# A convolution and a maxout layer on one core: both products in 64-row tiles of the array, side by side

## The chip, the core and the metric

The kernel runs on one core of a Trainium2 chip. The metric is the time of one execution on the device in microseconds (us); less is better. A core has five engines that run on their own queues: TensorE (PE, the products; its weight loads are listed as PEld), VectorE (DVE), ScalarE (ACT), GpSimd (POOL) and SyncE (SP, here only for issuing transfers). TensorE writes its products to PSUM, eight banks of 512 f32 columns on 128 partitions; VectorE and ScalarE read PSUM; everything else lies in SBUF.

## The reference

```python
# x: (8, 4160, 192), weight: (8 heads, 7 taps), moe_w1..3: (192, 768), moe_w_out: (768, 192)
w = softmax(weight, axis=-1)
x_pad = concat([zeros(B, 6, D), x], axis=1)
conv = einsum('hk,bskhg->bshg', w, windows_of_7(x_pad))     # causal, one filter per head of 24 channels
y = conv.reshape(33280, 192)
h = maximum(maximum(y @ w1, y @ w2), y @ w3)
out = h @ w_out                                             # (33280, 192) float32
```

## The kernel before

The 33280 tokens are cut into 65 blocks of 512 (`NBLK`); a block from the end of the eight sequences is put together from eight pieces of 64 tokens. Channels lie on partitions, tokens on columns. All products are in f16, with sums in f32.

The maximum is rewritten. With d1 = w1 - w3 and d2 = w2 - w3, max(y w1, y w2, y w3) is max(relu(y d1), y d2) + y w3, and the last term goes through w_out without a nonlinearity, as y m with m = w3 w_out. So l1, the first stage, needs two products in place of three, and st2, the second, adds y m to h w_out.

For each block t:

- `load_x` (issued on SP) brings x in chunks of 128 rows that overlap by 6 (122 new tokens each), and `cast_x` (GpSimd, L127) makes them f16.
- `conv` (L221): each chunk is multiplied with a band matrix of one head's taps, eight heads, five chunks, 40 products. Each works in one 128-row, 32-column tile of the array (`tile_position`). Two PSUM banks `G0`, `G1` hold four heads each. A head has 24 channels and takes a slot of 32 partitions, so the 192 channels fill two half tiles of 128 partitions, in which 8 of 32 rows of weights are zeros. ScalarE copies both banks to f16 (`y`, L228).
- `l1(t, j)` (L238) for six chunks j of 128 columns of the 768: two PSUM banks, for d1 and d2, and for each the two half tiles of channels in turn: 4 products of 128 rows and 512 columns. ScalarE takes relu of the first bank (`r`, L241), VectorE the maximum of r and the second bank (`h`, L242). Two buffers for each bank.
- `st2(t, s)` for four slices s of 128 tokens: two products y m (L253) and six h w_out (L256), 128 rows and 192 columns each, summed in one bank; two slices share a bank, and VectorE copies them out (L259).
- `store` (L268, L273) is issued on SP.

The order of the work is written out by hand, and engines take their instructions in that order. In a block's turn TensorE does l1 chunk 0, the conv of the next block, l1 chunk 1, and then in turn a slice of st2 of the block before and an l1 chunk, to chunk 5. In the first block's turn `make_m` computes m, with w3 transposed on TensorE in f32 (L198, L204). Ahead of that: the taps go to a band through a DRAM buffer `Rd` (L137 to L154); w1, w2, w3 come in pieces of 24 rows into the slots (L167, L170), w1 and w2 through ScalarE's queue, w3 through SP's, and are subtracted (`wd`, L186).

## Time and profile before

| | |
|---|---|
| median of 3 runs | 598.8 us (597.6 to 599.57) |
| the profiled execution | 599.25 us; its span in the trace 597.4 us |
| TensorE, VectorE, ScalarE, GpSimd busy | 94%, 57%, 50%, 12% of the span |
| mean granted TensorE clock | 0.997 |
| bytes moved by DMA | 61.40 MB, mean 103 GB/s |

The profile is one execution. A row of the groups names a line of the kernel, an engine, an operation, the tiles written and read, and a count; then the busy time in us and the mean duration of one in ns; then the idle time of the engine just before these instructions and what ended it. Records of matmuls overlap, since the next begins while the last drains, so the sum of their durations is more than the time that they take. The chain is followed back from the last instruction, at each step to what released it. A timeline row has a start and a length in us, an engine (ACTq and SPq are the issuing of a transfer), a line, an operation and a count of merged instructions.

### The profile page before, as it was taken

What the parts mean: (1) busy time and instruction counts of PE and PEld (TensorE: products, weight loads), DVE (VectorE), ACT (ScalarE), POOL (GpSimd) and SP (SyncE); (2) the same over time, 40 slices, a digit from 0 to 9 for tenths busy, and PEclk for the clock granted to TensorE, in tenths of its full rate; (3) what the DMA queues carried; (4) which work ended last, traced back from release to release, by engine and by line L of the source; (5) the groups of instructions that cost most, each with busy time, mean ns of one, the idle gap of its engine ahead of it and who ended that gap; (6) DMA issues with size and microseconds to landing.
All of it is one profiled execution on the core that took longest, in us unless ns stands there. A gap on an engine that the chain in (4) does not pass through costs nothing.

```text
span 597.4 us, 15039 instructions
## 1 busy us (share of the span) xinstructions
PE 562.2 (94%) x6300; PEld 361.1 (60%) x6300; DVE 342.9 (57%) x542; ACT 299.2 (50%) x523; POOL 72.0 (12%) x95
## 2 busy tenths in 40 slices
PE   0199999999999999999999999999999999999995
PEld 0066666666666666666666666666666666666663
DVE  1645656555655565556555656565555656565663
ACT  1135555555555555555555555555555555555551
POOL 2200111101111011101101111011101110111100
PEclk9999999999999999999999999999999999999998
DMA  7502432333234323442344334323443343324211
GB/s 206 172 1 61 119 109 83 109 120 112 83 105 120 114 87 100 121 118 83 98 121 120 86 94 120 120 87 92 121 121 89 91 119 112 103 86 118 83 55 53
DMA packets 79107, 61.40 MB, mean 103 GB/s; under 512 B 2912, under 2 KB 78208, under 8 KB 79040
## 3 DMA queue, kind: packets, MB, share of 16 engines
q1 hardware_dynamic: 78032, 58.43, 33.3%
q10 hardware_dynamic: 1008, 2.02, 1.0%
q8 instruction: 49, 0.80, 0.6%
q14 instruction: 18, 0.15, 0.1%
HBM read 34.34 MB, written 26.09 MB: 101 GB/s over the span
## 4 chain that ended last, share of the span: by engine, by line
PE 94%; DMA 3%; DVE 1%; ACT 1%; ACTq 0%; issue 0%; SPq 0%
PE l L238 58%; PE pso L256 22%; PE pso L253 7%; PE G L221 6%; DMA xf<-in_x_dram 1%; PE pm L204 1%; DMA ws<-in_moe_w_dram 1%; DMA wk<-in_weight_dram 1%; DMA Rd<-R 1%; ACTq L170 0%; DVE h L242 0%; DVE ws L167 0%; ACT r L241 0%; ACT wo L189 0%; SPq L116 0%
## 5 line engine op out<-in xcount | busy, mean ns | idle before, releaser
L238 PE MATMUL l<-y,wd 128*128 128x512 f16 x1560 | 392.4, 381 | 9.0 <-ACT y L228 9.0
L242 DVE TENSOR_TENSOR h<-r,l 128x512 f16<-128x512 f16 x390 | 268.2, 688 | 224.8 <-ACT r L241 220.4
L241 ACT ACTIVATE r<-l 128x512 f16<-128x512 f32 x390 | 234.1, 600 | 235.2 <-PE l L238 235.2
L238 PEld LDWEIGHTS <-wd 128*128 128x128 f16 x1560 | 143.8, 98 | 121.2 <-DVE wd L186 9.6
L256 PE MATMUL pso<-wo,h 128*128 128x192 f16 x1560 | 171.4, 246 | 0.4 <-DVE h L242 0.4
L256 PEld LDWEIGHTS <-h 128*128 128x128 f16 x1560 | 132.7, 98 | 0.6 <-DVE h L242 0.6
L127 POOL CAST x<-xf 128x960 f16<-128x960 f32 (+3 forms) x88 | 70.0, 800 | 487.3 <-DMA xf<-in_x_dram 358.0
L253 PEld LDWEIGHTS <-y 128*128 128x128 f16 x520 | 50.8, 98 | 60.7
L253 PE MATMUL pso<-m,y 128*128 128x192 f16 x520 | 85.4, 246 | 0.0
L228 ACT CAST y<-G 128x512 f16<-128x512 f32 x130 | 69.8, 589 | 28.0 <-PE G L221 28.0
L259 DVE COPY o<-pso 128x384 f32<-128x384 f32 x130 | 71.6, 551 | 1.8 <-PE pso L256 1.8
L221 PEld LDWEIGHTS <-x 128*32 128x32 f16 (+2 forms) x2624 | 36.6, 98 | 45.5 <-issue 40.0
L221 PE MATMUL G<-band,x 128*32 128x122 f16 (+3 forms) x2624 | 43.1, 211 | 18.4 <-DVE band L154 18.4
L189 ACT CAST wo<-wos 128x1152 f16<-128x1152 f32 x1 | 1.2, 1152 | 21.6 <-DMA ws<-in_moe_w_dram 21.6
L154 DVE COPY band<-bandc 128x1072 f16<-128x1072 f16 x1 | 2.5, 2530 | 9.5 <-DMA bandc<-Rd 9.5
L186 DVE TENSOR_TENSOR wd<-ws,ws 128x768 f16<-128x768 f32 x4 | 3.8, 959 | 4.2 <-DMA ws<-in_moe_w_dram 4.2
L204 PE MATMUL pm<-wos,w3t 128*128 128x192 f32 x24 | 4.2, 330 | 0.0
L204 PEld LDWEIGHTS pm<-wos,w3t 128*128 128x128 f32 x24 | 3.9, 190 | 0.2 <-DVE w3t L199 0.2
L167 DVE MEMSET ws<- 128x1536 f32 x2 | 2.7, 1338 | 0.5 <-issue 0.3
L206 DVE CAST m<-pm 128x192 f16<-128x192 f32 x2 | 0.7, 357 | 3.1 <-PE pm L204 3.1
L198 PE MATMUL pt<-ident,ws 128*128 128x128 f32 x12 | 1.7, 277 | 0.7 <-DVE w3t L199 0.7
L141 DVE TENSOR_REDUCE wsum<-wexp 128x8 f32<-128x56 f32 x1 | 0.3, 251 | 3.2 <-ACT wexp L139 3.2
(14 smaller groups left out, 8.9 us busy)
## 6 DMA issues: line engine op xcount, KB each, us to landing
out_dram<-o SPq DMA_DIRECT2D x64, 384.0 KB
xf<-in_x_dram SPq DMA_DIRECT2D x48, 480.0 KB
xf<-in_x_dram SPq DMA_DIRECT2D x16, 384.0 KB
ws<-in_moe_w_dram ACTq DMA_DIRECT2D x16, 72.0 KB
xf<-in_x_dram SPq DMA_DIRECT2D x8, 96.0 KB
ws<-in_moe_w_dram SPq DMA_DIRECT2D x8, 72.0 KB
wos<-in_moe_w_out_dram SPq DMA_DIRECT2D x1, 576.0 KB
xf<-in_x_dram SPq DMA_DIRECT2D x8, 70.5 KB
```

The costliest lines, as they stand in the source:

```text
L127: nc.gpsimd.tensor_copy(out=x16[0:rl, q0:q1, :], in_=xf[0:rl, q0:q1, :])
L167: eng.memset(st[:], 0.0)
L186: nc.vector.tensor_sub(out=d16[:, half, :], in0=wa[:, half, :], in1=w3s[:, half, :])
L204: nc.tensor.matmul(ps[:], lhsT=w3t[:, j, half, :], rhs=wos[:, j, :], start=(j == 0), stop=(j == NJ - 1))
L221: nc.tensor.matmul(G[h // 4][32 * g:32 * g + 32, lo:hi], lhsT=x16[0:rlen, q, cb:cb + 32], rhs=band[0:rlen, h, cc:cc + hi - lo], start=True ...
L228: nc.scalar.copy(out=y[:, i, 0:N], in_=G[i][:, 0:N])
L238: nc.tensor.matmul(ps[i][:, 0:N], lhsT=wd[i][:, half, P * j:P * (j + 1)], rhs=y[:, half, 0:N], start=(half == 0), stop=(half == 1))
L241: nc.scalar.activation(out=r[:, 0:N], in_=ps[0][:, 0:N], func=AF.Relu)
L242: nc.vector.tensor_max(out=hs[t][:, j, 0:N], in0=r[:, 0:N], in1=ps[1][:, 0:N])
L253: nc.tensor.matmul(ps[:, s % 2, :], lhsT=y[:, half, sl], rhs=m16[:, half, :], start=(half == 0), stop=False)
L256: nc.tensor.matmul(ps[:, s % 2, :], lhsT=hT[:, j, sl], rhs=wo[:, j, :], start=False, stop=(j == NJ - 1))
L259: nc.vector.tensor_copy(out=outs[t][0][:, s - 1:s + 1, :], in_=ps[:])
```

## The change

- The 192 channels are three groups of 64. An array tile of 64 rows takes one group, and the array has two such tiles, on partitions 0 to 63 and 64 to 127. In l1 the upper half holds d1 and the lower d2 (`wd` is one tensor now): three products each, taken in turn, into two banks.
- st2's sum over rows is split between the halves into two banks (`po0`, `po1`): h's rows 0 to 63 and 64 to 127 of each of six chunks, and three products y m shared out so that two slices have 15 products each, 8 on one half and 7 on the other, changing sides. ScalarE copies one bank to SBUF (`a`) and VectorE adds the other to it, in place of one copy.
- The conv's slots have to be packed to dense groups of 64 and be there twice, on both halves. The conv's result goes to `ys` for two blocks together; ten transfers on SP move the pieces of heads to the upper half of `yd`, and one on GpSimd copies the upper half to the lower (`repack`). The first block's pieces go on three queues, twice each, without the duplicate; the second block is packed alone.
- The conv runs four blocks ahead (`AHEAD`) in place of one; four convs, `make_m` and two groups' repack now stand ahead of the first l1, and in a turn the conv of block t+4.
- Stores are issued on GpSimd. x has three f32 buffers, not four; r has four. PSUM: `psp` and `psq` two banks each for l1, `psw` four banks shared by the conv and st2.
- The band is made from a zeroed DRAM buffer into which only the taps are written; half of the copy that turns it is ScalarE's. Weights come in four transfers of 64 rows on SP (w3 twice), and there are three subtractions, not four. `make_m` has the dense layout, its transposes in 64-row tiles.

On TensorE, l1 chunk 4 of a block begins so before (`l0` and `l1` are the banks for d1 and d2, `wd0` and `wd1` the weights):

```order
L238 LDWEIGHTS wd0_161
L238 MATMUL l0_46_4_6883<-y_46_6683,wd0_161 128x512
L238 LDWEIGHTS wd0_161
L238 MATMUL l0_46_4_6883<-y_46_6683,wd0_161 128x512
L238 LDWEIGHTS wd1_164
L238 MATMUL l1_46_4_6884<-y_46_6683,wd1_164 128x512
```

In the changed kernel an l1 chunk ends and st2 begins so on TensorE (`lp` and `lq` are the two banks of l1, `po0` and `po1` those of st2):

```order
L273 LDWEIGHTS wd_146
L273 MATMUL lp_32_1_6632<-yd_17_6045,wd_146 128x512
L273 LDWEIGHTS wd_146
L273 MATMUL lq_32_1_6633<-yd_17_6045,wd_146 128x512
L303 LDWEIGHTS yd_16_5658
L303 MATMUL po0_31_0_6643<-m16_154,yd_16_5658 128x192
L303 LDWEIGHTS yd_16_5658
L303 MATMUL po1_31_0_6644<-m16_154,yd_16_5658 128x192
```

Before, one bank was filled and then the other; now the banks take turns from product to product, in both stages.

On ScalarE, a block's turn before, from the last chunk of the block ahead of it:

```order
L241 ACTIVATE r_39_5_5909<-l0_39_5_5903 128x512
L241 ACTIVATE r_40_0_5925<-l0_40_0_5919 128x512
L228 CAST y_41_5970<-G0_41_5928 128x512
L228 CAST y_41_5970<-G1_41_5929 128x512
L241 ACTIVATE r_40_1_5979<-l0_40_1_5973 128x512
L241 ACTIVATE r_40_2_5997<-l0_40_2_5991 128x512
L241 ACTIVATE r_40_3_6015<-l0_40_3_6009 128x512
```

And in the changed kernel (`ys` is the conv's result in slots, `a` the copy of st2's first bank):

```order
L277 ACTIVATE r_31_0_6385<-lp_31_0_6377 128x512
L231 CAST ys_18_6242<-G0_35_6388 128x512
L231 CAST ys_18_6242<-G1_35_6389 128x512
L277 ACTIVATE r_31_1_6452<-lp_31_1_6444 128x512
L277 ACTIVATE r_31_2_6480<-lp_31_2_6472 128x512
L307 COPY a_30_1_6498<-po0_30_0_6455 128x384
L277 ACTIVATE r_31_3_6509<-lp_31_3_6501 128x512
L277 ACTIVATE r_31_4_6537<-lp_31_4_6529 128x512
L307 COPY a_30_3_6555<-po0_30_2_6512 128x384
L277 ACTIVATE r_31_5_6566<-lp_31_5_6558 128x512
```

The two casts of the conv stay between chunk 0 and chunk 1; two copies `a` are new, behind chunks 2 and 4.

GpSimd had only casts before. In the changed kernel its queue over two blocks is (`yd<-yd` is the duplicate, `out_dram<-o` a store):

```order
L133 CAST x_12_1717<-xf_1527 128x960
L260 DMA yd_1776<-yd_1776 64x3072
L317 DMA out_dram<-o_1532 128x4x192
L133 CAST x_13_1916<-xf_1715 128x960
L317 DMA out_dram<-o_1720 128x4x192
```

Each duplicate stands between a cast and a store, and each cast behind a store.

The core of the diff:

```diff
-    xfp = ctx.enter_context(tc.tile_pool(name="xfp", bufs=4))
+    xfp = ctx.enter_context(tc.tile_pool(name="xfp", bufs=3))
...
+    ysp = ctx.enter_context(tc.tile_pool(name="ysp", bufs=2))
+    ydp = ctx.enter_context(tc.tile_pool(name="ydp", bufs=4))
+    rp = ctx.enter_context(tc.tile_pool(name="rp", bufs=4))
     hp = ctx.enter_context(tc.tile_pool(name="hp", bufs=2))
+    tp = ctx.enter_context(tc.tile_pool(name="tp", bufs=2))
...
-    psg = ctx.enter_context(tc.tile_pool(name="psg", bufs=1, space=bass.MemoryType.PSUM))
-    psl = ctx.enter_context(tc.tile_pool(name="psl", bufs=2, space=bass.MemoryType.PSUM))
-    pst = ctx.enter_context(tc.tile_pool(name="pst", bufs=2, space=bass.MemoryType.PSUM))
+    psp = ctx.enter_context(tc.tile_pool(name="psp", bufs=2, space=bass.MemoryType.PSUM))
+    psq = ctx.enter_context(tc.tile_pool(name="psq", bufs=2, space=bass.MemoryType.PSUM))
+    psw = ctx.enter_context(tc.tile_pool(name="psw", bufs=4, space=bass.MemoryType.PSUM))
+    groups = [[0], [1]] + [list(range(t, min(t + 2, NB))) for t in range(2, NB, 2)]
+    group_of = {t: (g, k) for g, ts in enumerate(groups) for k, t in enumerate(ts)}
+    AHEAD = 4
...
+    zero = const.tile([P, BW], FP16)
+    nc.vector.memset(zero[:], 0.0)
+    Rd = dram.tile([P, BW], FP16)
+    nc.scalar.dma_start(out=Rd[:], in_=zero[:])
...
+    taps = const.tile([P, KW, NHEAD], FP16)
...
+        nc.vector.tensor_mul(out=taps[:, KW - 1 - k, :], in0=wexp[:, k, :], in1=wrec[:])
+    nc.scalar.dma_start(
+        out=bass.AP(tensor=Rd[:].tensor, offset=Rd[:].offset,
+                    ap=[[BW + NHEAD, P], [1, KW * NHEAD]]),
+        in_=taps[:].rearrange("p k h -> p (k h)"))
...
+    nc.scalar.dma_start(out=bandc[:].rearrange("p c h -> p (c h)"), in_=Rd[:])
...
+    HALF, NC = 64, D // 64
+    ws = const.tile([P, NC, DFF], FP32)
+    w3s = const.tile([P, NC, DFF], FP32)
+    for (lo, st, wsrc) in ((0, ws, moe_w1), (0, w3s, moe_w3), (HALF, ws, moe_w2), (HALF, w3s, moe_w3)):
+        nc.sync.dma_start(out=st[lo:lo + HALF, :, :], in_=wsrc.rearrange("(c r) f -> r c f", r=HALF))
...
+    wd = const.tile([P, NC, DFF], FP16)
+    for c in range(NC):
+        nc.vector.tensor_sub(out=wd[:, c, :], in0=ws[:, c, :], in1=w3s[:, c, :])
+    band = const.tile([P, NHEAD, BAND_W], FP16)
+    hh = NHEAD // 2
+    nc.vector.tensor_copy(out=band[:, 0:hh, :].rearrange("p h c -> p c h"), in_=bandc[:, :, 0:hh])
+    nc.scalar.copy(out=band[:, hh:NHEAD, :].rearrange("p h c -> p c h"), in_=bandc[:, :, hh:NHEAD])
...
+            for k in range(2):
+                js = slice(P * (2 * g + k), P * (2 * g + k + 1))
+                for c in range(NC):
+                    nc.tensor.transpose(ps[:, k, HALF * c:HALF * (c + 1)], w3s[0:HALF, c, js],
+                                        ident[0:HALF, 0:HALF])
+            nc.vector.tensor_copy(out=w3t[:, 2 * g:2 * g + 2, 0:D], in_=ps[:])
+            nc.vector.tensor_copy(out=w3t[:, 2 * g:2 * g + 2, D:2 * P], in_=ps[:, :, P:D])
...
+        G = [psw.tile([P, NBLK], FP32, tag="w", name=f"G{i}_{t}") for i in range(2)]
...
-        y = yp.tile([P, 2, NBLK], FP16, tag="y", name=f"y_{t}")
+        g, k = group_of[t]
+        if k == 0:
+            slots[g] = ysp.tile([P, 2, 2 * NBLK], FP16, tag="ys", name=f"ys_{g}")
         for i in range(2):
-            nc.scalar.copy(out=y[:, i, 0:N], in_=G[i][:, 0:N])
-        ys[t] = y
+            nc.scalar.copy(out=slots[g][:, i, NBLK * k:NBLK * k + N], in_=G[i][:, 0:N])
         xin.pop(t)
...
+    def repack(t):
...
+        if t >= NB or t != groups[group_of[t][0]][-1]:
+            return
+        g, k = group_of[t]
+        yd = dense[g] = ydp.tile([P, NC, 2 * NBLK], FP16, tag="yd", name=f"yd_{g}")
+        w = slice(0, NBLK * (k + 1))
+        if g == 0:
+            qs = (nc.sync, nc.scalar, nc.gpsimd)
+            todo = [(lo, p) for p in pieces for lo in (0, HALF)]
+            for n, (lo, (half, s0, c, r0, rows)) in enumerate(todo):
+                qs[n % 3].dma_start(out=yd[lo + r0:lo + r0 + rows, c, w],
+                                    in_=slots[g][s0:s0 + rows, half, w])
+            return
+        for (half, s0, c, r0, rows) in pieces:
+            nc.sync.dma_start(out=yd[r0:r0 + rows, c, w], in_=slots[g][s0:s0 + rows, half, w])
+        nc.gpsimd.dma_start(out=yd[HALF:P, :, w], in_=yd[0:HALF, :, w])
...
     def l1(t, j):
         N = blkN[t]
-        y = ys[t]
-        ps = [psl.tile([P, NBLK], FP32, tag=f"l{i}", name=f"l{i}_{t}_{j}") for i in range(2)]
-        for i in range(2):
-            for half in range(2):
-                nc.tensor.matmul(ps[i][:, 0:N], lhsT=wd[i][:, half, P * j:P * (j + 1)],
-                                 rhs=y[:, half, 0:N], start=(half == 0), stop=(half == 1))
+        g, k = group_of[t]
+        y = dense[g]
+        ps = [pool.tile([P, NBLK], FP32, tag=tag, name=f"l{tag}_{t}_{j}")
+              for pool, tag in ((psp, "p"), (psq, "q"))]
+        for c in range(NC):
+            for i in range(2):
+                row = slice(HALF * i, HALF * (i + 1))
+                nc.tensor.matmul(ps[i][:, 0:N], lhsT=wd[row, c, P * j:P * (j + 1)],
+                                 rhs=y[row, c, NBLK * k:NBLK * k + N],
+                                 start=(c == 0), stop=(c == NC - 1))
         r = rp.tile([P, NBLK], FP16, tag="r", name=f"r_{t}_{j}")
         nc.scalar.activation(out=r[:, 0:N], in_=ps[0][:, 0:N], func=AF.Relu)
         nc.vector.tensor_max(out=hs[t][:, j, 0:N], in0=r[:, 0:N], in1=ps[1][:, 0:N])
...
-        y, hT = ys[t], hs[t]
-        sl = slice(P * s, P * (s + 1))
+        g, k = group_of[t]
+        hT, y = hs[t], dense[g]
         if s % 2 == 0:
-            outs[t][1] = pst.tile([P, 2, D], FP32, tag="pso", name=f"pso_{t}_{s}")
-        ps = outs[t][1]
-        for half in range(2):
-            nc.tensor.matmul(ps[:, s % 2, :], lhsT=y[:, half, sl], rhs=m16[:, half, :],
-                             start=(half == 0), stop=False)
-        for j in range(NJ):
-            nc.tensor.matmul(ps[:, s % 2, :], lhsT=hT[:, j, sl], rhs=wo[:, j, :],
-                             start=False, stop=(j == NJ - 1))
+            halves[t] = [psw.tile([P, 2, D], FP32, tag="w", name=f"po{i}_{t}_{s}")
+                         for i in range(2)]
+        ps = halves[t]
+        tok = slice(NBLK * k + P * s, NBLK * k + P * (s + 1))
+        todo = []
+        for i in range(2):
+            row = slice(HALF * i, HALF * (i + 1))
+            mm = [(y[row, i, tok], m16[row, 0, :])]
+            if s % 2 == i:
+                mm.append((y[row, 2, tok], m16[row, 1, :]))
+            mm += [(hT[row, j, P * s:P * (s + 1)], wo[row, j, :]) for j in range(NJ)]
+            todo.append(mm)
+        for n in range(NJ + 2):
+            for i in range(2):
+                if n < len(todo[i]):
+                    nc.tensor.matmul(ps[i][:, s % 2, :], lhsT=todo[i][n][0], rhs=todo[i][n][1],
+                                     start=(n == 0), stop=(n == len(todo[i]) - 1))
         if s % 2 == 1:
-            nc.vector.tensor_copy(out=outs[t][0][:, s - 1:s + 1, :], in_=ps[:])
+            a = tp.tile([P, 2, D], FP32, tag="a", name=f"a_{t}_{s}")
+            nc.scalar.copy(out=a[:], in_=ps[0][:])
+            nc.vector.tensor_add(out=outs[t][:, s - 1:s + 1, :], in0=a[:], in1=ps[1][:])
     def store(t):
         if t < 0:
             return
-        ob = outs.pop(t)[0]
+        ob = outs.pop(t)
...
+                nc.gpsimd.dma_start(out=out[g0:g0 + n, :].rearrange("(s p) c -> p s c", p=P),
...
     assert all(n == NBLK for n in blkN)
-    conv(0)
-    for t in range(NB + 1):
-        if t < NB:
+    for t in range(AHEAD):
+        conv(t)
+        repack(t)
+        if t + 3 <= AHEAD + 1:
             load_x(t + 3)
-            cast_x(t + 2)
-            hs[t] = hp.tile([P, NJ, NBLK], FP16, tag="h", name=f"h_{t}")
-            outs[t] = [outp.tile([P, 4, D], FP32, tag="o", name=f"o_{t}"), None]
-            l1(t, 0)
-            conv(t + 1)
-            l1(t, 1)
-            for j in range(2, NJ):
-                st2(t - 1, j - 2)
-                l1(t, j)
-            if t == 0:
-                make_m()
-        else:
-            for s in range(4):
-                st2(t - 1, s)
+        if t + 3 <= AHEAD:
+            cast_x(t + 3)
+        if t == 1:
+            make_m()
+    for t in range(NB):
+        load_x(t + AHEAD + 2)
+        cast_x(t + AHEAD + 1)
+        hs[t] = hp.tile([P, NJ, NBLK], FP16, tag="h", name=f"h_{t}")
+        outs[t] = outp.tile([P, 4, D], FP32, tag="o", name=f"o_{t}")
+        l1(t, 0)
+        conv(t + AHEAD)
+        repack(t + AHEAD)
+        l1(t, 1)
+        for j in range(2, NJ):
+            st2(t - 1, j - 2)
+            l1(t, j)
         store(t - 1)
+    for s in range(4):
+        st2(NB - 1, s)
+    store(NB - 1)
```

More of the change, by code (lines that the diff above doesn't have):

```diff
@@ L194, in make_m @@
         for g in range(NJ // 2):
[L195 to L202 removed]
+            ps = psq.tile([P, 2, D], FP32, tag="q", name=f"pt{g}")
@@ L214, in conv @@
         N = blkN[t]
-        G = [psg.tile([P, NBLK], FP32, tag=f"g{i}", name=f"G{i}_{t}") for i in range(2)]
+        G = [psw.tile([P, NBLK], FP32, tag="w", name=f"G{i}_{t}") for i in range(2)]
         x16 = xin[t][1]
```

68 lines of the change are left out of this document (18 added, 50 removed).

## The prediction

> **What bounds the kernel now.** I read the page first: who is busy, and whose work makes up the chain that ended last.
>
> ```profile
> PE 562.2 (94%) x6300; PEld 361.1 (60%) x6300; DVE 342.9 (57%) x542; ACT 299.2 (50%) x523; POOL 72.0 (12%) x95
> PE 94%; DMA 3%; DVE 1%; ACT 1%; ACTq 0%; issue 0%; SPq 0%
> GB/s 206 172 1 61 119 109 83 109 120 112 83 105 120 114 87 100 121 118 83 98 121 120 86 94 120 120 87 92 121 121 89 91 119 112 103 86 118 83 55 53
> ```
>
> TensorE is 94% of the chain, DMA 3%. The stretches of the span say whether TensorE ever pauses in the middle (its columns: length, TensorE busy, weight loads, VectorE, ScalarE, GpSimd, clock, DMA share, GB/s):
>
> ```profile
> 100.00:580.00 480.00, 480.00 (x5428) 307.77 (x5427) 285.56 (x452) 256.95 (x451) 57.99 (x75) 1.00 0.35 102
> ```
>
> 480.00 of 480 us at clock 1.00: no gap. A busy matmul row overlaps its neighbour, so the real price of one is read from the chain in order of time, one block of 512 tokens long (start, length, work):
>
> ```profile
> 51.25 1.73 PE l L238 x8
> 52.98 0.58 PE G L221 x40
> 53.56 0.97 PE l L238 x4
> 54.53 0.17 PE pso L253 x2
> 54.69 0.49 PE pso L256 x6
> 55.19 0.86 PE l L238 x4
> ...
> 59.76 1.73 PE l L238 x8
> ```
>
> A block takes 59.76 - 51.25 = 8.51 us. A 512-column product costs 1.73/8 = 0.216 us, a 192-column one (0.17 + 0.49)/8 = 0.0825 us, the conv's 40 small products 0.58 us, and there is 0.97 - 0.86 = 0.11 us behind the conv. Sum: 24 x 0.216 + 32 x 0.0825 + 0.58 + 0.11 = 5.18 + 2.64 + 0.69 = 8.51. TensorE's stream is the bound, and nothing else.
>
> **TensorE's work after.** One l1 chunk had 4 products in turn; now it has 6 of 64 rows, three on each half of the array: if the two halves run side by side, 3 x 0.216 = 0.65 us instead of 0.86. One st2 slice had 8 products in turn, now 15 in two halves, 7.5 x 0.0825 = 0.62 us instead of 0.66. The conv keeps its shape, and the array changes its tile shape twice in a block as before. Sum: 18 x 0.216 + 30 x 0.0825 + 0.69 = 3.89 + 2.48 + 0.69 = **7.05 us**, 1.46 less.
>
> No row shows 64-row tiles. The nearest is the conv: 40 products of up to 122 columns, four column tiles, in 0.58 us, 58 ns for a round of four. At 0.0825 us for 192 columns one such product alone is about 0.052 us, so four at once cost about 6 ns more than one. Bounds for a pair: 1.0 to 2.0 products; I take 1.0, the row that is nearest. The Trainium skill, *TensorE: Matmul & The Clock Gate*, "Measured speedup vs the span model", gives 3.07 for four row tiles, not 4; a pair at that efficiency would cost 1.30 products and the block, by estimate, 8.97 us. By it this change loses (the second rival); the trace agrees only in part: the conv's row shows 4 x 52/58 = 3.6 of four, though of column tiles.
>
> The second unknown is weight loads: 136 in a block instead of 96. The groups by shape:
>
> ```profile
> L238 PEld LDWEIGHTS <-wd 128*128 128x128 f16 x1560 | 143.8, 98 | 121.2 <-DVE wd L186 9.6 <-issue 2.5
> L221 PEld LDWEIGHTS <-x 128*32 128x32 f16 x2496 | 35.1, 98 | 45.0 <-issue 39.5 <-POOL x L127 5.5
> L198 PEld LDWEIGHTS pt<-ident,ws 128*128 128x128 f32 x12 | 1.4, 140 | 1.1 <-DVE w3t L199 0.9
> ```
>
> A 128-column f16 load is recorded as long as a 32-column one (98 ns), and the f32 load of 128 columns longer (140). So the f16 load occupies little more than the conv's, which follow each other at 0.58/40 = 14.5 ns. I cost the loads at nothing, hidden under the products; the upper bound is the first rival.
>
> **What then comes late: the way out of PSUM.** Both l1 halves now end together, and pools `psp` and `psq` have two buffers each, so l1 chunk j+2 waits until VectorE has read chunk j. Durations and gaps:
>
> ```profile
> L242 DVE TENSOR_TENSOR h<-r,l 128x512 f16<-128x512 f16 x390 | 268.2, 688 | 224.8 <-ACT r L241 220.4 <-PE l L238 4.4
> L241 ACT ACTIVATE r<-l 128x512 f16<-128x512 f32 x390 | 234.1, 600 | 235.2 <-PE l L238 235.2
> L228 ACT CAST y<-G 128x512 f16<-128x512 f32 x130 | 69.8, 589 | 28.0 <-PE G L221 28.0
> L259 DVE COPY o<-pso 128x384 f32<-128x384 f32 x130 | 71.6, 551 | 1.8 <-PE pso L256 1.8
> ```
>
> ```profile
> 300.29 1.07 ACT L228 CAST y<-G 128x512 f16<-128x512 f32 x2 [0.42 <-PE G L221]
> 301.25 0.61 ACT L241 ACTIVATE r<-l 128x512 f16<-128x512 f32 x1
> 302.97 0.69 DVE L242 TENSOR_TENSOR h<-r,l 128x512 f16<-128x512 f16 x1 [0.39 <-ACT r L241]
> 303.23 1.03 PE L238 MATMUL l<-y,wd 128*128 128x512 f16 x4
> 303.57 0.55 DVE L259 COPY o<-pso 128x384 f32<-128x384 f32 x1
> 303.86 0.60 ACT L241 ACTIVATE r<-l 128x512 f16<-128x512 f32 x1 [0.93 <-PE l L238]
> 304.49 0.69 DVE L242 TENSOR_TENSOR h<-r,l 128x512 f16<-128x512 f16 x1 [0.37 <-ACT r L241]
> ```
>
> r's bank is full after two products, at 303.23 + 0.43 = 303.66; r starts at 303.86, 0.20 later; h starts 0.03 after r. From h's end to TensorE the only case is in the last block:
>
> ```profile
> 587.61 0.69 DVE L242 TENSOR_TENSOR h<-r,l 128x512 f16<-128x512 f16 x1 [0.37 <-ACT r L241]
> 588.35 0.26 PE L256 MATMUL pso<-wo,h 128*128 128x192 f16 x1 [0.40 <-DVE h L242]
> ```
>
> 0.05. So from an l1's start until its buffers are free: 0.65 + 0.20 + 0.60 + 0.03 + 0.69 + 0.05 = 2.22 us. Between most chunks j and j+2 there stand one l1 more and two st2: 2 x 0.65 + 2 x 0.62 = 2.54, enough. Where only one st2 stands (chunk 4, st2, chunk 5, next block's chunk 0) it is 1.92: TensorE waits **0.30 us**. The next pair then has 0.65 + 0.95 + 0.69 = 2.29, enough. Chunk 1's r stands on ScalarE behind the two y casts (spaced (301.25 - 300.29)/2 = 0.48): its h ends about 2.5 us after the conv, when chunk 3 begins at 2.53: just in time. Before, the same places had 0.86-us l1s and an r that began 0.43 us earlier, so nothing waited.
>
> The other new evacuation work fits: ScalarE gets two copies of 128x384 (at 0.55 like the VectorE copy of that size) beside eight of 0.6 spaced 0.48, about 4.9 us a block; VectorE two adds in place of two copies of that size (0.55 to 0.69 each), at the measured spacing of 0.60 after an h about 4.9. Neither reaches 7. The conv and st2 now share four banks; the nearest release is st2's first pair, whose banks the last add of the block before leaves some 1.5 us earlier by the same steps. Bounds of the stall: 0 (period 7.05) to 0.65 (7.7; chunk 3 late as well); I take 0.30 plus 0.02 for pairs, **7.37 us**.
>
> **The repack.** Every second block SP issues 10 moves that wait for y, and GpSimd one duplicate that waits for all ten; the stores go from SP to GpSimd. Issue prices of 24-row moves, and landing of one (from the chain):
>
> ```profile
> 19.90 6.73 ACTq L170 DMA_DIRECT2D ws<-in_moe_w_dram  x16
> 52.50 0.45 SPq L116 DMA_DIRECT2D xf<-in_x_dram  x1
> ```
>
> ```profile
> 20.50 1.98 DMA ws<-in_moe_w_dram
> ```
>
> Ten issues x 0.42 = 4.2 us, 2.0 to land, the duplicate about as much again (0.45 + 2 to 4), y casts 1.3: about 10 to 12 us after the conv. It is needed at the first l1 of the third block behind, 2.7 x 7.37 = 20 us later: hidden, 8 us to spare. Queued behind the moves on SP is the load of x for two blocks later; behind the duplicate on GpSimd a store and the next cast, used one block later: hidden too. One x buffer less costs nothing: the cast that frees it was done two blocks before. No row shows a DMA issued by GpSimd; SP's 0.45 is the nearest, and with casts near 1 us a 7.4-us block leaves GpSimd room for several us. Bytes for two blocks: x 0.98 MB, out 0.79, moves 0.79: 2.56 MB in 14.7 us, 174 GB/s, below the 206 of the first slice.
>
> **Both ends.** Before, block 2's l1 begins at 51.25 + 0.86 = 52.1. After, the rows are:
>
> ```profile
> 15.77 2.53 DVE L154 COPY band<-bandc 128x1072 f16<-128x1072 f16 x1 [9.51 <-DMA bandc<-Rd]
> 18.35 1.05 PE L221 MATMUL G<-band,x 128*32 128x122 f16 x40 [18.35 <-DVE band L154]
> 23.86 0.96 DVE L186 TENSOR_TENSOR wd<-ws,ws 128x768 f16<-128x768 f32 x1 [2.38 <-DMA ws<-in_moe_w_dram]
> 31.46 0.99 POOL L127 CAST x<-xf 128x960 f16<-128x960 f32 x1 [10.47 <-PE G L221]
> 39.44 4.17 PE L204 MATMUL pm<-wos,w3t 128*128 128x192 f32 x24
> ```
>
> The band's copy on VectorE stands behind three wd subtractions, and these behind four weight loads: 0.5 + 2.4 + 0.5 MB at 206 GB/s is 16.5 us; 3 x 0.96 and half of 2.53 make 21: conv(0) about 2.5 us later than 18.35. Casts to 23.5, seven moves on each of three queues to 26.5. Meanwhile conv(1) and make_m (transposes about 2.5 us, 4.17 us of products) fill TensorE to about 31, so first l1 near 32. Then conv(4) waits for its cast, which stands on GpSimd behind block 1's duplicate (SP: a load, ten moves, landing: about 33.5; cast near 35.7). Five l1 without st2 at 2.22/2 = 1.1 us: 42; block 1: 7.4. **Block 2 begins at about 49.5** (46 to 54). At the end:
>
> ```profile
> 589.89 5.02 SPq L273 DMA_DIRECT2D out_dram<-o  x8
> 590.63 0.56 DVE L259 COPY o<-pso 128x384 f32<-128x384 f32 x1 [0.76 <-PE pso L256]
> ```
>
> From the last st2 (52.1 + 63 x 8.506 + 2.64 = 590.6) to the span's end were 6.8 us; the copy and eight GpSimd issues make about 7.8 (6.5 to 11).
>
> **Sum.** 49.5 + 63 x 7.37 + 2.5 + 7.8 = 524; the last four blocks have no conv, which gives 1 back: span 523. The profiled execution took 599.25 us for a span of 597.4, 1.85 more, and the median of the runs is 598.8, so about 525 us.
>
> **Rivals.** (1) *Weight loads bind st2; slower.* In st2 they follow each other every 82.5 ns and no f16 row shows 128-column loads closer. If that were a load's own time, 60 loads make 60 x 0.0825 = 4.95 us, the block 3.89 + 4.95 + 0.69 = 9.53, plus 65 x 1.02: about 665 us. It decides from 65 ns a load (3.89 + 60p + 0.69 = 8.51). Against it: equal 98-ns records at 32 and 128 columns. The Trainium skill, same page, "LDWEIGHTS", puts a load at columns/1.2 ns whatever the rows, 107 ns here, which would be slower still; the trace disagrees, 82.5 ns holds a load and a product. (2) *The halves share something and overlap only in part, or not at all*: the change does not do what it says; slower. It decides from (8.51 - 0.69)/6.37 = 1.23 products a pair; at 1.30 the block is 6.37 x 1.30 + 0.69 = 8.97 us, about 626 us in all; at 2.0 it is 13.4 us, about 918. For it: no row with row tiles; against it: the conv's rounds at 58 ns. The page's 3.07 named above is such a case. (3) *Evacuation binds throughout*: if a copy or cast is always in front of r, 2.22 + 0.48 = 2.70 for two chunks, 8.1 us a block, about 570 us. The Trainium skill, *TensorEngine Tiling (Array Packing)*, "PSUM Bottleneck", warns of this: tiling speeds up TensorE, not the reading of PSUM. For it: my 2.22 against 2.54 is thin. (4) *The repack's way is longer than its lead*: at 25 us the block becomes 25/2.7 = 9.3, about 647 us; it loses from 2.7 x 8.51 = 23 us. Against it: 10 to 12 us from the rows.
>
> **Numbers.** Forecast 0.70, its own range 501 (period 7.05, start 46) to 553 (7.7, start 54). Rival 3: 0.12; rival 1: 0.05; rival 2: 0.07; rival 4: 0.04; gains that just cancel: 0.02. The range 500 to 572 takes the first two, 0.82. Faster by over 0.3%, about what runs of this kernel can tell: 0.82; the same 0.02; slower 0.16 (rivals 1, 2, 4).
>
> **What would show it.** In the chain a block of 7.0 to 7.7 us; l1 chunks of 0.65 and st2 of 0.62; one wait of TensorE on h at the block's border, 0.3 us; no waits for the dense y. If l1 takes 1.3 us, rival 2; if l1 is 0.65 but st2 near 1.2, rival 1; waits on h at every chunk, rival 3; first l1 of a pair waiting for a DMA, rival 4.

## The result, and the profile after

The changed kernel takes 539.03 us (median of 4 runs, 538.25 to 539.29) against 598.97 us before (4 runs beside it): a ratio of 0.900, 95% interval 0.8982 to 0.9018. The forecast was 525.0 (500 to 572), faster: the sign and the range hold, the point is 14 us low. The profiled execution's span is 537.5 us. From the page of the changed kernel (busy time; TensorE's busy tenths in 40 slices; the chain that ended last):

```profile
PE 491.3 (91%) x8906; PEld 348.1 (65%) x8906; DVE 337.7 (63%) x542; ACT 362.0 (67%) x654; POOL 143.4 (27%) x205
PE   0084999999999999999999999999999999999993
PE 86%; DMA 6%; ACT 2%; SPq 2%; POOL 1%; DVE 1%; issue 1%; ACTq 1%; POOLq 0%
```

TensorE is still the bound, but 86% of the chain instead of 94%: in the first four slices (54 us) it is busy for 0, 0, 8 and 4 tenths. So there are two readings to make, the steady block and the run-up. First the steady block, in the chain in order of time:

```profile
303.69 0.58 PE po L303 x15
304.27 0.21 PE lp L273
...
304.92 0.21 PE lp L273
305.13 0.34 PE lq L273
...
305.90 0.58 PE G L222 x31
306.48 0.32 PE lp L273
...
313.28 0.58 PE G L222 x36
```

From conv to conv 313.28 - 305.90 = 7.38 us; the forecast was 7.37. An l1 chunk (six products) is three steps of 0.21 to 0.22 (chunk 5 here from 304.27 to 304.92). A slice of the second stage is booked as 0.58 here and as 0.66 in every other one, 0.62 in the mean, since its 15 products are 8 on one half and 7 on the other in turn. The 0.32 behind the conv holds the same 0.11 as before. The engines' own instructions around 305 show where the rest is (start, length, work; the first row is VectorE's reading of chunk 4):

```profile
304.36 0.69 DVE L278 TENSOR_TENSOR h<-r,lq 128x512 f16<-128x512 f16 x1 [0.62 <-ACT r L277]
304.54 0.38 PE L273 MATMUL lp<-yd,wd 64*128 64x512 f16 x1
304.54 0.38 PE L273 MATMUL lq<-yd,wd 64*128 64x512 f16 x1
304.76 0.38 PE L273 MATMUL lp<-yd,wd 64*128 64x512 f16 x1
305.10 0.37 PE L273 MATMUL lq<-yd,wd 64*128 64x512 f16 x1
```

The two halves start in the same 10 ns and follow each other at 0.216. The next block's chunk 0 starts on its upper half at 304.76, but on its lower half only at 305.10: its second PSUM bank is the one that VectorE reads for chunk 4, until 304.36 + 0.69 = 305.05, and the product starts 0.05 later, as the prediction took it from the last block of the kernel before. That is the wait at the block's border. The ten moves of the repack and their duplicate, in one period of two blocks (the engines' own instructions, and the page's row of landings, us at its end):

```profile
307.14 8.30 SPq L259 DMA_DIRECT2D yd<-ys  x10
317.70 0.55 POOL L260 DMA_DIRECT2D yd<-yd  x1 [10.02 <-DMA yd<-ys]
yd<-yd POOLq DMA_DIRECT2D x31, 384.0 KB, 6.2
```

The duplicate lands at about 317.70 + 6.2 = 323.9, 18 us after the conv at 305.83; the forecast had 10 to 12. It is needed three blocks after 304.9 or so, at about 327: 3 us of spare, not 8. Still hidden.

The run-up, in the chain:

```profile
7.30 9.38 DMA Rd<-taps
...
23.28 2.57 ACT band L187
...
41.44 4.01 DMA xf<-in_x_dram
45.60 1.00 POOL x L133
46.64 1.05 PE G L222 x39
...
61.20 0.34 PE lq L273
```

Block 2 begins at 61.2; the forecast said 49.5. That is 11.7 of the 14.5 us by which the span (537.5 against 523) was missed. Some late blocks (the 59 intervals from conv(5) to the last make 436.7 us, 1.3 over 59 x 7.38), 0.01 us in each of 63 blocks, and what is then left, about 1 us at the end, are the rest. The granted clock has a part in the run-up: it falls in TensorE's wait of 6.67 us ahead of conv(4) and is 0.50 from 42 to 50 us, so conv(4) takes 1.05 us there instead of 0.58 and a pair of products 0.42 instead of 0.21.

### The profile page after: what moved, and what is told of

It reads as the page before. It is cut to its first block, busy times and chain, and to the rows that moved or that the text cites. A ratio compares the mean times of both kernels' runs of the same rounds, so it can differ in the third digit from the quotient of the medians.

```text
span 537.5 us, 21248 instructions
## 1 busy us (share of the span) xinstructions
PE 491.3 (91%) x8906; PEld 348.1 (65%) x8906; DVE 337.7 (63%) x542; ACT 362.0 (67%) x654; POOL 143.4 (27%) x205
## 4 chain that ended last, share of the span: by engine, by line
PE 86%; DMA 6%; ACT 2%; SPq 2%; POOL 1%; DVE 1%; issue 1%; ACTq 1%; POOLq 0%
PE lp L273 32%; PE po L303 29%; PE lq L273 18%; PE G L222 7%; DMA Rd<-taps 2%; SPq L259 2%; DMA bandc<-Rd 1%; DMA Rd<-zero 1%; ACTq L255 1%; DVE h L278 1%; ACT r L277 1%; DMA yd<-ys 1%; DMA xf<-in_x_dram 1%; POOL out_dram L322 1%; POOL x L133 1%
## 5 line engine op out<-in xcount | busy, mean ns | idle before, releaser
L278 DVE TENSOR_TENSOR h<-r,lq 128x512 f16<-128x512 f16 x390 | 268.3, 688 | 163.3 <-ACT r L277 150.6
L273 PE MATMUL lq<-yd,wd 64*128 64x512 f16 x1170 | 316.5, 377 | 2.0 <-DVE h L278 2.0
L273 PE MATMUL lp<-yd,wd 64*128 64x512 f16 x1170 | 316.3, 378 | 0.0
L277 ACT ACTIVATE r<-lp 128x512 f16<-128x512 f32 x390 | 234.0, 600 | 117.6 <-PE lp L273 89.0
L303 PE MATMUL po<-wo,h 64*128 64x192 f16 x3120 | 182.9, 243 | 0.7 <-DVE h L278 0.7
L273 PEld LDWEIGHTS <-wd 64*128 64x128 f16 x2340 | 129.4, 94 | 79.2 <-issue 36.4
L303 PEld LDWEIGHTS <-h 64*128 64x128 f16 x3120 | 144.4, 94 | 1.0 <-DVE h L278 0.9
L231 ACT CAST ys<-G 128x512 f16<-128x512 f32 x130 | 69.8, 589 | 26.1 <-PE G L222 17.3
L303 PE MATMUL po<-m,yd 64*128 64x192 f16 x780 | 86.5, 243 | 0.0
L308 DVE TENSOR_TENSOR o<-a,po 128x384 f32<-128x384 f32 x130 | 71.1, 547 | 2.1 <-ACT a L307 2.1
```

Source lines behind the costliest of these rows:

```text
L231: nc.scalar.copy(out=slots[g][:, i, NBLK * k:NBLK * k + N], in_=G[i][:, 0:N])
L273: nc.tensor.matmul(ps[i][:, 0:N], lhsT=wd[row, c, P * j:P * (j + 1)], rhs=y[row, c, NBLK * k:NBLK * k + N], start=(c == 0), stop=(c == NC ...
L277: nc.scalar.activation(out=r[:, 0:N], in_=ps[0][:, 0:N], func=AF.Relu)
L278: nc.vector.tensor_max(out=hs[t][:, j, 0:N], in0=r[:, 0:N], in1=ps[1][:, 0:N])
L303: nc.tensor.matmul(ps[i][:, s % 2, :], lhsT=todo[i][n][0], rhs=todo[i][n][1], start=(n == 0), stop=(n == len(todo[i]) - 1))
L308: nc.vector.tensor_add(out=outs[t][:, s - 1:s + 1, :], in0=a[:], in1=ps[1][:])
```

## The experiments

**1. Are the halves side by side because of the order in which the products are issued?** The l1 loops are exchanged, so that each half's three products stand together in the program:

```diff
-        for c in range(NC):
-            for i in range(2):
+        for i in range(2):
+            for c in range(NC):
```

> Only l1's order of issue changes: the three products of the upper half first, then the three of the lower, so that program order no longer lets them stand side by side. Theory A (the halves overlap, but a product starts no sooner than the one ahead of it in the program): the lower half's first product starts with the upper half's third, at 0.43 us, a chunk takes 5 x 0.216 = 1.08 us in place of 0.65 and st2 falls into step behind it; the block goes from 7.38 to 8.4 to 9.3 us, about 600 to 660 us in all. Theory B (each half takes its products for itself, whatever the order): nothing changes, 7.38 us and 539 us. Theory C (what overlapped was only the records, and the halves work in turn): the same 7.38 as well, since the order would not matter.

Measured (one run): 538.97 us, a steady block of 7.38. TensorE's instructions:

```profile
304.88 0.38 PE L273 MATMUL lp<-yd,wd 64*128 64x512 f16 x1
304.90 0.38 PE L273 MATMUL lq<-yd,wd 64*128 64x512 f16 x1
```

The lower half's first product starts 20 ns after the upper half's first, though two upper ones stand ahead of it in the program. Each half takes its own products; the side-by-side order in the code does nothing for the time here. This run alone leaves theory C standing, which forecasts the same time; experiments 10 and 11 exclude it.

**2. Is the wait at the border the release of PSUM?** The last two slices are cut, so that 7.5 products stand between chunk 5 and the next chunk 0, and none of the work changes:

```diff
-        for j in range(2, NJ):
-            st2(t - 1, j - 2)
-            l1(t, j)
+        st2(t - 1, 0)
+        l1(t, 2)
+        st2(t - 1, 1)
+        l1(t, 3)
+        st2(t - 1, 2, 0)
+        l1(t, 4)
+        st2(t - 1, 2, 1)
+        st2(t - 1, 3, 0)
+        l1(t, 5)
+        st2(t - 1, 3, 1)
```

> The same products in the same sums; only the places where the stream of st2 is cut change, to 15, 15, 7.5, 15 and 7.5 products, so that one piece stands between chunk 5 and the next block's chunk 0 as well. Theory A (the 0.33 us a block above the sum of products is chunk 0 waiting for VectorE to leave the banks of chunk 4, 2.22 us after chunk 4 began): every chunk then has at least 2.22 us, the block goes from 7.38 to about 7.07 us, 63 x 0.31 = 20 us less, about 519 us. Theory B (the 0.33 us is a price of back-to-back chunks, of tile changes or of alternating halves): no change, 539 us, within 3.

Measured: 524.39 us, ratio 0.8738 (0.8695 to 0.8780). The chain:

```profile
302.97 0.58 PE G L222 x36
...
309.12 0.26 PE po L301 x7
309.37 0.21 PE lp L273
...
310.02 0.58 PE G L222 x36
```

7.05 us a block, and chunk 0 runs in even steps from 309.37 to 310.02. The wait was 7.38 - 7.05 = 0.33 us; what is left is the bare sum of the products. The cut also parts chunk 5 from the next chunk 0, so the time alone would fit a price of chunks that follow each other as well; that it is the bank shows in VectorE's row above. 63 blocks of 0.33 are 20.8 us; the profiled execution (span 517.8) shows 19.7 of them, the median of the runs (519.54 to 525.35) only 14.6. In the profiled execution, the fastest of the four, late blocks make the difference: with a shorter block, the conv more often waits for its x cast. The other three have no trace, so what made them 4 to 6 us longer is not shown. The conv's line in the trace (what TensorE sat idle for, us and times, with the run-up; 29.0 us and 16 times in the changed kernel):

```profile
  POOL x L133: 33.8, 24
```

**3. Loads and casts of the run-up ahead of the moves.** One edit: repack behind load_x and cast_x instead of ahead of them.

> In the run-up ahead of the first l1 only: the loads of blocks 3 to 5 and the casts of 3 and 4 are issued ahead of the moves of the repack and not behind them. Theory A (the run-up is late because conv(3) and conv(4) wait for x that stands on SP's and GpSimd's queues behind moves of 0.75 us each): conv(4) follows the first l1 without its wait of 6.7 us, the clock does not fall, the first l1 comes some 2 us earlier, and then block 1 waits for its duplicate, which is as late as before: block 2 begins 5 to 9 us earlier, 530 to 534 us. Theory B (the run-up is set by the bytes of weights and by make_m): less than 2 us.

Measured: 539.57 us, ratio 0.9014 (0.8995 to 0.9033), no gain. conv(4) came 8 us earlier (38.64 instead of 46.64), but conv(5) then waited, and it begins at 53.84. The queues of SP and GpSimd ahead of it:

```profile
42.66 7.59 SPq L259 DMA_DIRECT2D yd<-ys  x10
52.27 0.53 POOL L260 DMA_DIRECT2D yd<-yd  x1 [7.66 <-DMA xf<-in_x_dram]
52.79 0.99 POOL L133 CAST x<-xf 128x960 f16<-128x960 f32 x1
```

The cast stands behind the duplicate on GpSimd, and the duplicate waits for the tenth move, issued at 50.2. The wait moved by one block.

**4. The band ahead of the weights.** Weights and w_out go to ScalarE's queue behind the band's transfers, and the band's copies ahead of the wd subtractions:

```diff
-        nc.sync.dma_start(out=st[lo:lo + HALF, :, :], in_=wsrc...)
+        nc.scalar.dma_start(out=st[lo:lo + HALF, :, :], in_=wsrc...)
```

> In the run-up: the weights and w_out go on ScalarE's queue behind the band's load, and the band's copy on VectorE goes ahead of the subtractions. Theory A (the write of the taps took 9.4 us because 2.4 MB of weights were ahead of it on the DMA engines): it takes 2 to 4 us, conv(0) begins at 15 to 17 us and not at 25, the weights come by 27, and block 2 begins 5 to 9 us earlier: 530 to 534 us. Theory B (128 writes of 112 bytes to DRAM are slow by themselves): the taps take 9 us again, conv(0) begins near 22, the weights later than now, no gain or a loss up to 5 us: 537 to 545 us.

Measured: 538.75 us, ratio 0.8985 (0.8962 to 0.9007), no gain. The chain:

```profile
7.20 3.17 DMA Rd<-taps
...
12.88 13.36 DMA w3s<-in_moe_w_dram
```

The 14 KB of taps take 3.2 us instead of 9.4: they had stood behind 2.4 MB of weights. The band is back from DRAM 10 us earlier (its copy begins at 13.1 instead of 23.3), and conv(0) begins at 14.5 instead of 25.05. But the weights now land at 26.2, with make_m and conv(2) behind them, and conv(4) is nearly where it was, at 46.01 instead of 46.64.

**5. Fewer moves in the run-up.** Edit 3, and blocks 0 and 1 repacked as one pair:

```diff
-    groups = [[0], [1]] + [list(range(t, min(t + 2, NB))) for t in range(2, NB, 2)]
+    groups = [list(range(t, min(t + 2, NB))) for t in range(0, NB, 2)]
```

> The changed kernel with loads and casts of the run-up ahead of the moves, and blocks 0 and 1 repacked together: 30 moves in the run-up instead of 40, 17 of them on SP instead of 27. Theory A (SP's serial issue of moves at 0.75 us, and the duplicate and cast behind it, set when block 2 begins): SP is done 7.5 us earlier and conv(5) and block 2 come 5 to 8 us earlier: 531 to 535 us. Theory B (the run-up is bound elsewhere: the weights, make_m, the transfers): 538 to 541 us. Theory C (block 0 waits for block 1's conv and casts, and this only shifts the start): first l1 3 us later and block 2 earlier by less, 536 to 538 us.

Measured: 538.25 us, ratio 0.8985 (0.8955 to 0.9015): the median is in theory B's range, though two of the four runs (536.26 and 536.79) are in theory C's. The chain of the profiled execution, the slowest of the four:

```profile
36.30 1.06 PE G L222 x71
...
45.53 2.16 DMA yd<-ys
...
48.31 0.54 POOL yd L260
48.85 1.00 POOL x L133
49.90 1.05 PE G L222 x39
```

conv(2) and conv(3) stand on TensorE behind make_m, so SP's ten moves for blocks 2 and 3 begin at 38.5 instead of 42.55, 4 us earlier and not the 7.5 that ten fewer issues would allow; then moves, duplicate, cast and conv(5) follow as before. The conv in block 2's turn is 2.4 us earlier (59.55 against 61.97). Four later blocks of 8.1 to 8.9 us, whose conv came late behind its x cast, took it back. Theory A's mechanism is there; its price was too high, since one edit only hands the run-up to the next chain.

**6. All of it together**, and what 3 and 5 showed: make_m behind conv(3), and loads and casts of x one block earlier throughout:

```diff
-        if t + 3 <= AHEAD + 1:
+        if t + 3 <= AHEAD + 2:
             load_x(t + 3)
-        if t + 3 <= AHEAD:
+        if t + 3 <= AHEAD + 1:
             cast_x(t + 3)
-        if t == 1:
+        repack(t)
+        if t == AHEAD - 1:
             make_m()
...
-        load_x(t + AHEAD + 2)
-        cast_x(t + AHEAD + 1)
+        load_x(t + AHEAD + 3)
+        cast_x(t + AHEAD + 2)
```

> Five edits together: the second stage cut into 15, 15, 7.5, 15 and 7.5 products between the l1 chunks; the taps written ahead of the weight loads; blocks 0 and 1 repacked as one pair (30 moves in the run-up instead of 40); loads and casts of x one block earlier; make_m behind conv(3). Theory A (what was lost against the forecast lies in the run-up, where SP's issue of moves at 0.75 us each sets the end, and at the block's border): weights land near 26, make_m to 35, first l1 near 36, block 2's l1 near 49 instead of 61.2, a steady block of 7.05 us with fewer late casts: 512 us, 507 to 519. Rival B (the run-up has another bound behind the moves, for one the transfers themselves or the weights): only the cut pays, as it did alone, 522 to 526 us. Rival C (moves of a pair finish later than block 0 and 1's separate ones and the first l1 waits longer): first l1 at 42 or later, 520 us and up.

Measured: 511.73 us, ratio 0.8542 (0.8529 to 0.8555): 27 us below the changed kernel, and the fastest of the study. The chain:

```profile
13.12 16.06 DMA w3s<-in_moe_w_dram
...
40.54 0.32 PE lp L273
...
302.94 0.58 PE G L222 x37
...
309.99 0.58 PE G L222 x40
```

The conv's line again, what TensorE sat idle for:

```profile
  POOL x L133: 10.8, 14
```

7.05 us a block; 63 x 0.33 = 20.8 of the 27 us. The conv in block 2's turn comes at 56.07 instead of 61.97: 5.9 us. No block behind conv(6) is over 7.25: the loads that lead by a block more have ended the late casts. The run-up is not as short as expected (first l1 at 40.5, not 36; block 2 near 55.3, not 49): the weights landed 3 us later than I took, with make_m behind them, at a granted clock of 0.50 up to 38 us. So the time was right by luck: a run-up 6 us too long, and an expected 512 that left as much more room behind block 2 than the kernel needed.

**7. And make_m under the weight loads.** Upper w3 and w_out load first, and the first pair's moves go out on SP and GpSimd alone:

```diff
+    load_w(0, w3s, moe_w3)
+    nc.scalar.dma_start(out=wos[:], in_=moe_w_out...)
+    for args in ((0, ws, moe_w1), (HALF, ws, moe_w2), (HALF, w3s, moe_w3)):
+        load_w(*args)
...
-            qs = (nc.sync, nc.scalar, nc.gpsimd)
+            qs = (nc.sync, nc.gpsimd)
```

> The kernel with all gains, and three edits more in its run-up: the upper half's w3 and w_out load ahead of the other weights, so that the transposes and products of make_m (8.6 us behind the last weight there) run under the loading of the rest, with the subtractions for wd behind them; the pair 0 moves go out on SP and GpSimd alone, ten each, since ScalarE's seven stood behind 2.4 MB of weights and took 15.3 us to issue; ScalarE's y casts for blocks 2 and 3 come that much earlier. Theory A (first l1 at 40.5 is set by the last weight and make_m behind it): weights still land near 29, wd 32, but the pair's moves land near 37 and bind then; first l1 near 37, moves of pair 1 done near 50, block 2's l1 near 51 instead of 55.4: 507 us, 504 to 510. Rival B (moves through the shared transfer engines, slowed by the weights, bind whatever the order): 510 to 514 us, first l1 at 40 or later.

Measured: 512.03 us, ratio 0.8565 (0.8539 to 0.8591): no gain over the last. The first l1 did come at 36.22, but the chain goes on:

```profile
51.38 2.21 DMA yd<-ys
53.59 0.45 PE lq L275
...
54.89 0.98 PE G L224 x35
```

Block 2 waits for its own repack until 53.6, and its conv then takes 0.98 us instead of 0.58. The window behind (busy times of the engines; granted clock, DMA share and GB/s last):

```profile
55.00:57.00 2.00, 2.00 (x46) 1.21 (x40) 0.69 (x1) 1.34 (x3) 0.00 (x0) 0.50 0.47 95
```

The granted clock is 0.50 after each such wait, here and at 36 to 40. Theory A had the first l1 right, but block 2's l1 came at 53.6 instead of 51, and the half clock took what that still left of the gain: the conv in block 2's turn begins at 54.89 instead of 56.07, 1.2 us earlier than in experiment 6, and the next conv comes 8.12 us behind it instead of 7.05. The time is rival B's, the first l1 is not.

**8. How thin is the repack's cover?** One number, AHEAD = 3 instead of 4.

> AHEAD = 3: the conv and the repack lead the first product by one block less, 2 x 7.38 - 1.3 = 13.5 us for a pair instead of 20.8. Theory A (y casts, ten moves at 0.73 us, the duplicate and its landing take 17.5 us, as the trace of the changed kernel has them in its steady part): TensorE waits about 4 us in every second block, mean block (17.5 + 1.3)/2 = 9.4 us, 655 us, 630 to 690; the wait stands in front of a pair's first l1 and ends with the duplicate's landing. Rival B (the prediction's 10 to 12 us): hidden still, 535 to 542 us.

Measured (one run): 651.62 us, the 59 intervals from conv(5) to the last 9.3 us in the mean. The chain:

```profile
301.57 5.74 DMA yd<-yd
...
307.36 0.60 PE lq L273
```

A pair's first l1 waits for the duplicate's landing; TensorE's waits of this kind add up to 83.7 us in 30 places. The clock falls behind some of them (0.933 in the mean instead of 0.985), which has a part in the 113 us lost. The way is the 17 to 18 us of the trace; the prediction's 10 to 12 would have stayed hidden.

**9. Does "all but the conv" matter?** The second stage back in the whole array, one bank and one copy; three products of y with m on the upper 64 rows, six on 128:

```diff
-            mm = [(y[row, i, tok], m16[row, 0, :])]
-            if s % 2 == i:
-                mm.append((y[row, 2, tok], m16[row, 1, :]))
-            mm += [(hT[row, j, P * s:P * (s + 1)], wo[row, j, :]) for j in range(NJ)]
+        todo = [(y[0:HALF, c, tok], m16[:, c, :]) for c in range(NC)]
+        todo += [(hT[:, j, P * s:P * (s + 1)], wo[:, j, :]) for j in range(NJ)]
```

> Second stage in the whole 128-row array, l1 still in halves: per slice three 64-row products of y with m and six 128-row products, 9 in turn in one bank instead of 15 in two halves; one VectorE copy instead of a ScalarE copy and an add. A slice is 9 x 0.0825 = 0.74 us instead of 0.62, four make 0.49 us more a block; chunk 0's wait shrinks from 0.30 to 0.18. Theory A (a change of the tile shape costs nothing by itself): 7.05 + 0.49 + 0.18 = 7.72 us a block, 561 us, 553 to 567. Theory B (each change of shape costs 0.055 to 0.11 us, as the 0.11 behind the conv suggests; 6 to 8 more of them in a block): 0.4 to 0.9 us more, 8.0 to 8.5 us a block, 580 to 610 us. Theory C (ScalarE's and VectorE's evacuation still had a part in the 7.38, and one copy less relieves it): under 7.5 us, below 548 us.

Measured: 606.68 us, ratio 1.0136 (1.0119 to 1.0153): 1.4% above the kernel before, with l1 still in halves. TensorE's instructions:

```profile
303.29 0.41 PE L294 MATMUL po<-m,yd 64*128 64x192 f16 x3
303.63 0.67 PE L294 MATMUL po<-wo,h 128*128 128x192 f16 x6
304.23 0.39 PE L273 MATMUL lp<-yd,wd 64*128 64x512 f16 x1
```

Three products take 0.34 us up to the first 128-row one, where 3 x 0.0825 = 0.25 was the sum: 0.09 more. Six take 0.60 up to the next 64-row one, against 0.495: 0.105 more. Eight such changes make 0.8 us a block; from conv to conv it takes 8.41 us (298.89 to 307.30 in the chain): theory B. The halved second stage brings little of its own (0.62 against 0.66 a slice); its worth is that the array keeps its tiles.

**10. What does a 64-row product cost alone?** All l1 products of both maxout inputs on rows 0 to 63 (so w1 - w3 makes both):

```diff
-                row = slice(HALF * i, HALF * (i + 1))
+                row = slice(0, HALF)
```

> All six products of an l1 chunk on rows 0 to 63 (both maxout inputs are then made from w1 - w3, so the output is not the reference's); the rest as in the changed kernel. Theory A (a 64-row product alone costs as much as a full one, 0.216 us, and the pair runs wholly side by side): a chunk takes 6 x 0.216 = 1.30 us, the block 7.05 + 18 x 0.216 = 10.94 us with no wait at its border, 63 x 3.56 more than 539: 763 us, 750 to 775. Theory B (a lone 64-row product is shorter, and the pair overlaps only in part): a block between 8 and 10.5, 580 to 735 us.

Measured (one run): 1429.78 us. The page, and the chain:

```profile
PE 1387.0 (97%) x8906; PEld 691.5 (48%) x8906; DVE 349.2 (24%) x542; ACT 370.0 (26%) x654; POOL 143.8 (10%) x205
PEclk9555555555555555555555555555555555555555
```

```profile
705.54 0.43 PE lp L273
705.97 0.43 PE lq L273
```

Products in turn, at 0.427 us and a clock of 0.50: 0.2135 in full-clock terms, and the block of 721.87 - 700.61 = 21.3 us is 10.6. Theory A holds in cycles: alone, 64 rows cost what 128 do, so the pair's overlap is whole. Experiment 11 shows the same at full clock: there the six products of a chunk on one half start from 300.90 to 301.98, 0.216 us apart. No theory had the clock: TensorE, 97% busy, stayed at half.

**11 and 12. Why half the clock?** Once with only chunks 0, 2 and 4 on one half, once with all l1 products on rows 64 to 127 (outputs changed in the same way):

```diff
-                row = slice(HALF * i, HALF * (i + 1))
+                row = slice(HALF * i * (j % 2), HALF * (i * (j % 2) + 1))
```

> l1 chunks 0, 2 and 4 with all six products on rows 0 to 63 (their output is not the reference's), chunks 1, 3 and 5 as pairs; the rest as in the changed kernel. The kernel with all l1 products on one half stayed at clock 0.50 from 51 us on, though TensorE's row said 97% busy. In full-clock terms a block there is 36 x 0.216 = 7.78 us of half an array and 3.17 us of the rest, 64% of the array in the mean; here it is 3.89 + 1.94 + 3.17 = 9.0 us with 78%. Theory A (the granted clock follows how much of the array works, and one half with short stretches of pairs is too little, three pairs of chunks are enough): clock 1.00, 9.0 us a block, 63 x 1.62 more than 539: 641 us, 630 to 655. Theory B (any run of products on one half alone, 1.3 us here, takes the clock down for good): clock 0.50, 18 us a block, about 1210 us. Theory C (the clock there was low for a reason of that run alone): as A here, and the question stays open.

> All six products of an l1 chunk on rows 64 to 127 instead of 0 to 63 (the output is not the reference's). Theory A (the granted clock follows how much of the array works; 64% in the mean is too little, 78% was enough): clock 0.50 again and about 1430 us. Theory C (the clock of 0.50 was a matter of that one run): clock near 1.00, 10.9 us a block, 763 us.

Measured (one run each): 641.09 us, the number worked out to the microsecond, at clock 1.00 in the steady part; and 1430.13 us at a mean clock of 0.516. So the low clock was no accident of one run, nor a matter of which half. One window of the first of the two:

```profile
100.00:600.00 500.00, 500.00 (x7574) 324.45 (x7573) 290.32 (x447) 306.73 (x556) 115.16 (x159) 1.00 0.52 141
```

In all three runs the clock falls to 0.50 at 40 to 43 us, in the same wait of the run-up as in the changed kernel (not at 51 us, as I had it). With 78% of the array at work it came back at about 52 us; with 64%, and TensorE as busy, it did not come back before the last blocks' end, at about 1420 us. So the granted clock does not go with TensorE's busy time alone; that it goes with how much of the array works fits these three runs. Whether 64% would also bring a full clock down, where between the two it turns, and over what time it is counted, was not tried. The Trainium skill, *TensorE: Matmul & The Clock Gate*, "Part 1: The HAM clock gate", says that the clock is released by how busy TensorE has been, after some 3.4 us of sustained activity. The half clock behind the second wait of experiment 7, about 3.4 us by its windows (0.94 in 52 to 54 us, 0.50 in 54 to 56, 0.70 in 56 to 58), agrees; a row of 97% busy at 0.50 would agree if the gate counted the working part of the array, which no run here shows directly.

## Why the prediction was right, and where it was not

- **A pair of 64-row products at 1.0 product, the step that carried the gain: right.** 18 x 0.216 + 30 x 0.0825 + 0.69 = 7.05 was forecast as TensorE's stream, and experiments 2 and 6 ran at 7.05. The conv's row of four column tiles was the right neighbour; still, 1.0 was the best end of bounds from 1.0 to 2.0, with no row of such tiles to decide it. The 1.30 worked out from the Trainium skill, *TensorE: Matmul & The Clock Gate*, "Measured speedup vs the span model", does not hold for two row tiles of 64 rows here; rival 2 falls.
- **Weight loads at nothing: right.** 7.05 leaves no room for them; rival 1 falls.
- **Two changes of tile shape a block, as before, so nothing new: right**, and it was worth more than the text knew: 0.09 to 0.105 us a change (experiment 9).
- **The wait at the border, 0.30 us: right in place and mechanism, 0.33 in size.** It stood where only one slice covers the release chain, ended 0.05 us after VectorE's h, and went when 7.5 products were moved there. Rival 3 (evacuation binding at every chunk) falls.
- **The repack: hidden as said, but mis-sized.** The ten issues were priced at 0.42 us, an average over ScalarE's queue. SP's take 0.83 with the gaps between them. The duplicate's landing takes 6.2 us, not 2 to 4. Spare is 3 us, not 8; a lead of one block less costs 113 us (experiment 8), so rival 4 was 3 us away.
- **The run-up, "block 2 begins at about 49.5": the step that failed.** 61.2 was measured. Stage by stage the run fell behind by 4.2 us at conv(0) (25.05 instead of 20.9), 7.1 at the first l1 (39.1 instead of 32), 10.9 at the end of conv(4)'s cast (46.6 instead of 35.7) and 11.7 at block 2. conv(0) was taken 2.5 us later than before, from bytes ahead of the band's copies; the taps' small write behind the weights, 9.4 us, was not seen, and conv(0) came at 25 instead of 21. The moves' low price then hid that SP issues 27 of them one after another, from 27.5 to 50.6, with loads, duplicate and casts queued in between; and the forecast had full clock throughout, where conv(4) and the pairs behind it ran at 0.50. Experiments 3, 4 and 5 each met the next chain; all edits together, the cut of the second stage among them, gave 5.9 us. How the 11.7 us divide between the causes is therefore not settled by the runs.

## What to carry to other kernels

Two 64-row tiles ran wholly side by side here, and a second stage of 128-row products between them cost all of the gain; count the changes of shape, and do not leave one half idle for most of the time. When TensorE's stream gets shorter, look for the place where the least work stands between the last reader of a PSUM buffer and its next writer, and move half a stage there: here that was 0.33 us of every block, with not a product fewer. Price a DMA's issue by the row of its own queue, and check a run-up chain by chain, since the second-latest chain takes over at once.

## What the runs showed of the hardware that I had not expected

- Products for the other half of the array start ahead of their place in the program: 20 ns after the first instead of behind three of them (experiment 1).
- A change between 64-row and 128-row tiles cost 0.09 to 0.105 us each (experiment 9).
- With all l1 products on one half the granted clock, once fallen in the run-up, stayed at 0.50 (window 100 to 1400 us) although TensorE was 97% busy; with every second chunk so, it came back and was 1.00 (window 100 to 600 us; experiments 10 to 12).
- A 14 KB write took 9.4 us with 2.4 MB of weights on their way, and 3.2 us ahead of them (experiment 4).
